# Reordering the first batch of an attention and feed-forward kernel: part one's plain products first, q and k of part two in one load each, two heads in other banks

## The chip, the cores and the metric

The kernel runs on one core of a Trainium2 chip. A core has TensorE (matrix products, results in PSUM), VectorE and ScalarE (elementwise work; both read PSUM), GpSimd and SyncE (here memory clearing and the issue of DMAs). PSUM has eight banks of 128 partitions by 512 float32 values. The metric is device time in microseconds (us) of one execution: the median of several runs. Lines of the profile call TensorE PE, VectorE DVE, ScalarE ACT, GpSimd POOL and SyncE SP; PEld is TensorE's load of weights.

## What is computed

Eight batches of eight heads attend over 576 tokens of 64 values, and a feed-forward network with a squared relu follows. Heads 0 to 3 ("plain") see the last 32 tokens; heads 4 to 7 ("dilated") see every fourth of the last 128.

```python
# B, H, S, D = 8, 8, 576, 64; window 32, dilation 4
scores = q @ k.T / sqrt(D)
rel = pos[:, None] - pos[None, :]
mask_plain = (rel >= 0) & (rel < 32)
mask_dil = (rel >= 0) & (rel < 128) & (rel % 4 == 0)
attn = softmax(where(mask_plain if h < 4 else mask_dil, scores, -1e9))
x = (attn @ v).transpose(0, 2, 1, 3).reshape(4608, 512)   # B*S tokens, H*D wide
h = maximum(x @ w_in, 0)                                  # w_in 512 x 2048
out = (h * h) @ w_out                                     # w_out 2048 x 512, float32
```

## The kernel before

Heads go in pairs e = 0 to 3 (two heads of 64 values fill 128 partitions); e = 0 and 1 are plain, 2 and 3 dilated. Tokens are grouped in fours: token 4m + r has residue r and index m, m from 0 to 143. Batch 0 is cut in two parts: part one (0 in the code) is m below 64, that is 256 tokens, part two (1 in the code) the other 320. The normalised attention output goes, transposed, into `xT`, whose 512 rows are four blocks kt = 0 to 3, one for each head pair. The feed-forward network takes tokens in tiles: four of 256, then 512 each.

Instructions are issued on each engine in the order in which the code writes them. For the start that order is written out by hand in the string `PROGRAM` (lines 21 to 36). It is cut by "|": all codes before the first "|" run ahead of the first group of feed-forward work, the codes of the next stretch after group 0, and so on. In the first stretch the codes mean, with e and part as digits:

- `L0:q023`, `L0:q10123`: load q and k of batch 0, a part and a list of head pairs, one DMA each from GpSimd (`load_qk`, line 156). `L0:v..` loads v, `L0:i` and `L0:o` quarters of w_in and w_out. A DMA issue on GpSimd waits for the landing of the one eight issues before it.
- `T`: transposes of q and k (line 505, into a tile `pa`). `C`: their copies out of PSUM, on VectorE, or for plain pairs with "a" the q half on ScalarE (lines 512 to 520); dilated pairs of part two have a small extra copy (`k8`, line 514).
- `B`: a product that puts the mask's bias in PSUM (line 535). `S`: scores (line 557). `E`: exponential on ScalarE (line 565), and for part two a product with the mask on VectorE (line 568).
- `h`: VectorE copies v of the plain heads of part one (tile `plain`, profile name `osb`, loaded from SyncE and ScalarE at line 745) to the place where it is used (line 803).
- `P`: the product with v (line 595). `D`: the sums of the exponentials (line 611). `L`, `X`: logarithm and exponential on ScalarE that give the reciprocal (lines 618 and 621). `M`: the product that normalises, on VectorE, into `xT` (line 628). For part one two head pairs share a pair of banks, and one `L`, `X`, `M` serves both.
- `wn`, `Wn`: n matrix products of zeros (line 475), whose results are not used; `W2+31` puts them on the bank of S31.

The four banks of the pool `ps_f` (profile name `pf`) serve B and S, some of P's results and the accumulators of the feed-forward network; `ps_a` has two banks (`pa`), `ps_o` and `ps_d` one each (`po`, `pd`). A tile that is allocated waits until the bank that it is given has been read for the last time.

A feed-forward tile is a list of groups (`ffn_groups`, line 653). A first-layer group g1(i) makes products over w_in (`mm1`, line 666; 676 in the profile), then ScalarE's relu (line 687) and VectorE's square (line 688); second-layer groups follow (line 711). For the tile of tokens 0 to 255, group 0 makes kt 0 and 1 of two accumulators and group 1 their kt 2 and 3. `P01` to `M31` of part two are issued after group 1. Then the groups of the first two tiles are interleaved: group 2 is the first of tokens 256 to 511 (g1(0)), groups 3 and 4 are g1(2) and g1(3) of tokens 0 to 255, group 5 is g1(1) of tokens 256 to 511, which completes the accumulators that group 2 began.

Of the kernel before, what the change touches and what calls it, by code (L numbers as in the profile page):

```python
# [18 lines left out]


PROGRAM = (
    "L0:q001 L0:q023 L0:q101 L0:q123 L0:v0d L0:i0 L0:v1p L0:v1dr L0:i1 L0:i2 L0:i3 L0:o0 L0:o1 L0:o2 L0:o3 "
    "L1:q00123 z y L1:v0dp L1:q10123 L1:v1dpr w9 T00 C00a T10 C10a B00 B10 W2 S00 E00 B20 W1 S10 E10 u B30 W3 "
    "T20q W6 T20k C20v T30 C30v h W3 S20 E20 W2 S30 E30 T01 C01v T11 C11a P00 P10 D00 D10 L00 T21 C21v T31 "
    "C31v S01 S11 X00 M00 E01 E11 P20 P30 D20 D30 L20 X20 M20 S21 S31 W2+31 E21 E31 | | P01 D01 L01 X01 M01 "
    "P11 D11 L11 X11 M11 P21 D21 L21 X21 M21 P31 D31 L31 X31 M31 | | | | | | | | | | | | | | | m n | | | | | "
    "L2:q00123 L2:q10123 | 1q1 1q3 | 1q2f 1k2f | 1k1a 1v3 | 1a2 | 1v2 1k0a 1q0v | 1o2 | 1a0 1a1 | 1k3 1o0 1o1f "
    "| 1a3 1Q0 | 1K0 1o3 | 1Q1 1K1 | 1Q2 | 1b0 | | 1Q3 1K2 L2:vwpdr L3:q00123 L3:q10123 | L2:x | | 2q0 | | 2k0 "
    "1V2 | 1b2 1p0 | 1b1 1V3 1K3 | | 1p2 1p1f | 2a0 1b3 | 2k1l 2o0 1p3f 2b0 2k1h | 2q1 2k2 L3:x | | 2q2 2p0 "
    "L3:vwpdr 2a1 | | | 2b1 | 2o1 2a2 2v2 2q3 | | 2p1f | 2k3 | 2b2 2o2 | 2v3 | 2a3 2p2f L4:q10123 | 2b3 2o3 | "  # L30
    "3k1 | 2p3 | 3q1v L4:q00123 | 3k0l | | 3a1 3k0h | | 3k2l | 3o1 3q0 | 3k2h 3v2 | | | 3a0 | 3b1 | 3q2 | | "
    "3p1 L4:x L4:vwpdr | | 3b0 | 3a2 3q3 3o0 3k3 | | | 3o2 3b2 | 4q1 | 3p0 3v3 | 3a3 | 3p2 4q2 4q0 | L5:q10123 "
    "3b3 4k0al | 3o3 4k0ah | 4k1 | | L5:q00123 3p3 4k2 4k3 4a0 L5:vwpdr | | | 4b0 | | 4q3 | | 4o0 | | | 4a2 "
    "4v2 | 4b2 | 4a3 L5:x 4a1 | 4o2 | | | 4p2 L6:q00123 4v3 | | 4b1 | | 4p0 | | 4p1 | 5q0 5k0 | 4b3 | | | | "
    "4o1 | | 5k2 L6:q10123 4o3 | 5q2 5k1 | | 4p3 | 5q1 |"
)


# [25 lines left out]
def kernel(  # L64
# [414 lines left out]
    def first_step(code: str):  # L479
# [6 lines left out]
        m0, n = MS[part], MN[part]  # L486
# [4 lines left out]
        pair = (e - e % 2, 0) if part == 0 else (e, 1)  # L491

        def byr(ap):
            return ap.rearrange("p (r m) -> p r m", r=RES)

        if what == "T":
# [3 lines left out]
            x = first["T", e, part]  # L500
# [7 lines left out]
        elif what == "C":  # L508
            copy = nc.scalar.copy if code[3] == "a" else nc.vector.tensor_copy
            x = first.pop(("T", e, part))  # L510
# [25 lines left out]
        elif what == "S":  # L536
# [7 lines left out]
            y = 0  # L544
            for x, (i, r, q0, q1) in enumerate(bl):
                z = (q1 - q0) * (RES if r is None else 1)
# [15 lines left out]
        elif what == "E":  # L562
            ps = first.pop(("S", e, part))
            to = pts[e][:, c : c + ps.shape[1]]
            nc.scalar.activation(to, ps, ACT.Exp, scale=SCALE)
            if part:
                mask = (mask_d if dil else mask_p)[:, c : c + ps.shape[1]]
                nc.vector.tensor_tensor(out=to, in0=to, in1=mask, op=ALU.mult)
        elif what == "P":
            if ("P", *pair) not in first:  # L570
                if pair in ((2, 0), (0, 1), (3, 1)):
                    od = ps_o.tile([P, 512], f32, name="po"), ps_d.tile([P, 512], f32, name="pd")
                else:
                    pool, nm = (ps_a, "pa") if pair == (1, 1) else (ps_f, "pf")
                    od = [pool.tile([P, 512], f32, name=nm) for _ in range(2)]
                first.pop("W", None)
                first["P", *pair] = od
            o, d = [x[:, y0 : y0 + w] for x in first["P", *pair]]
            o3, d3 = byr(o), byr(d)
            pt = pts[e]  # L580
            bl = blocks(0, e, part)
            y, dms = c, []
            for x, (i, r, q0, q1) in enumerate(bl):
                z = (q1 - q0) * (RES if r is None else 1)
                quads = dil and i < 8
                for rows in sides if quads else [slice(0, P)]:
                    if r is None:
                        to, rhs = o3[rows, :, q0 - m0 : q1 - m0], byr(pt[rows, y : y + z])
                    else:
                        to, rhs = o3[rows, r, q0 - m0 : q1 - m0], pt[rows, y : y + z]  # L590
                    if quads:
                        lhs = vds[0][rows, e - NE // 2, i // RES, D * (i % RES) : D * (i % RES) + D]
                    else:
                        lhs = vbd[0][:, e, i, :]
                    nc.tensor.matmul(
                        to, lhs, rhs, start=(x == 0 and y0 == 0), stop=(x == len(bl) - 1), skip_group_check=True
                    )
                if not dil:
                    dms.append((d3[:, :, q0 - m0 : q1 - m0], byr(pt[:, y : y + z])))
                y += z  # L600
            if dil and part == 0:
                dms.append((d, pt[:, 0:w]))
            elif dil:
                main = byr(pt[:, c : c + 448])
                dms += [(d3, main[:, :, 32:112]), (d3[:, :, 0:32], main[:, :, 0:32]),
                        (d3[:, :, 64:80], byr(pt[:, c + 448 : c + 512]))]
            first["D", e, part] = dms
        elif what == "D":
            dms = first.pop(("D", e, part))
            for x, (dd, rh) in enumerate(dms):  # L610
                nc.tensor.matmul(
                    dd, ones, rh, start=(x == 0 and y0 == 0), stop=(x == len(dms) - 1), skip_group_check=True
                )
        else:
            n = 512 if part == 0 else w
            if what == "L":
                first["X", e, part] = rec = r_pool.tile([P, 512], f32, name="rec")
                nc.scalar.activation(rec[:, 0:n], first["P", e, part][1][:, 0:n], ACT.Ln)
            elif what == "X":
                rec = first["X", e, part][:, 0:n]  # L620
                nc.scalar.activation(rec, rec, ACT.Exp, scale=-1.0)  # L621
            else:
                o, rec = first["P", e, part][0][:, 0:n], first.pop(("X", e, part))[:, 0:n]
                to = xT[:, e, RES * m0 : RES * m0 + n]
                if part == 0:
                    to = xT[:, e : e + 2, 0:w]
                    o, rec = [x.rearrange("p (e n) -> p e n", e=2) for x in (o, rec)]
                nc.vector.tensor_tensor(out=to, in0=o, in1=rec, op=ALU.mult)  # L628
# [24 lines left out]
    def ffn_groups(tk0: int, nt: int):  # L653
# [6 lines left out]
        kts = (0, 2, 1, 3) if tk0 >= NT else (0, 1, 2, 3)  # L660
# [5 lines left out]
        def mm1(u, ks):  # L666
            if u not in acc:
                acc[u] = ps_f.tile([P, NT], f32, name="pf")
            for x in range(per):
                f = per * u + x  # L670
                piece = max(y for y in range(len(w_in_sb)) if w_cuts[y] <= P * f)
                c0 = 512 * (f // 4) + f % 4 - w_cuts[piece]
                for kt in ks:
                    for y0, y1 in cuts:
                        t0 = (tk0 + y0) % RING
                        nc.tensor.matmul(  # L676
                            acc[u][:, nt * x + y0 : nt * x + y1],
                            w_in_sb[piece][:, kt, c0 : c0 + 509 : 4],
                            xT[:, kt, t0 : t0 + y1 - y0],
                            start=(kt == kts[0] and x == 0 and y0 == 0),  # L680
                            stop=(kt == kts[-1] and x == per - 1 and y1 == nt),
                            skip_group_check=True,
                        )
            if ks[-1] != kts[-1]:
                return
            hv = h2[:, per * u : per * u + per, 0:nt]
            nc.scalar.activation(hv, acc[u][:, :].rearrange("p (x n) -> p x n", x=per), ACT.Relu)  # L687
            nc.vector.tensor_tensor(out=hv, in0=hv, in1=hv, op=ALU.mult)  # L688

        def g1(i):  # L690
            if i < 2 and tk0 < NT:
                for u in range(2):
                    mm1(u, kts[2 * i : 2 * i + 2])
            elif i < 2 and early:
                for u in (2 * i, 2 * i + 1):
                    mm1(u, kts[:cut])
            elif i < 4 and early:
                for u in (2 * i - 4, 2 * i - 3):
                    mm1(u, kts[cut:])
            else:  # L700
                mm1(i, kts)
# [189 lines left out]
```

## Time and profile before

| | |
|---|---|
| Median of 4 runs | 310.98 us (309.46 to 312.5) |
| The profiled execution | 310.02 us, its span 308.2 us |
| TensorE busy | 300.6 us, 98% of the span |
| VectorE, ScalarE, GpSimd busy | 194.1, 198.7, 93.8 us |
| First product over w_in of group 0 | 17.69 us from the span's start |
| First product over w_in of group 2 | 22.66 us |

A line of the timeline gives start and length in us, engine, line of the code, operation, what it writes and reads, shapes and count; in brackets stands how long the engine had been idle before it and what ended that. A line of waits gives who waited for whom, the time in total, how often, and the longest. A line of GpSimd with DMA_DIRECT2D is the issue of a transfer; its landing is told apart. Starts of matmuls that follow each other without a gap overlap their ends by up to 0.2 us, so lengths of neighbours don't add up; differences of starts do.

### The profile page before, as it was taken

Reading aid. Unit: us, or ns where it says so; the run is one execution under the profiler, and the core shown is the slowest. Engines: PE = TensorE matmul, PEld = TensorE weight load, DVE = VectorE, ACT = ScalarE, POOL = GpSimd, SP = SyncE. Lnnn points to the kernel's source line nnn. Section 1 sums busy time; section 2 is a strip of 40 time slices with the busy share of each in tenths; the row PEclk is TensorE's granted clock in tenths of the full one; section 3 lists DMA queues with packets and bytes.
Section 4 is the critical chain, followed back from the end, with each engine's and each line's share of the span. In section 5 each row is a group of like instructions: output and inputs, shape, how many; then the busy total and the mean of one; then the engine's idle time right before and its main releaser. Section 6 shows DMA issues by size and latency. Waiting matters only on the chain.

```text
span 308.2 us, 6774 instructions
## 1 busy us (share of the span) xinstructions
PE 300.6 (98%) x2532; PEld 187.9 (61%) x2564; DVE 194.1 (63%) x635; ACT 198.7 (64%) x425; POOL 93.8 (30%) x138
## 2 busy tenths in 40 slices
PE   8999999999999999999999999999999999999995
PEld 3679757868755555555599555555555555445544
DVE  1465566988988888885798479946994334104400
ACT  6686658859869868894488448854786456216511
POOL 8679685574255165301641051000000000000000
PEclk9999999999999999999999999999999999999999
DMA  7999999999989979999899976502200210121022
GB/s 105 194 140 213 207 160 170 183 159 220 142 147 192 173 113 212 137 121 163 118 123 136 149 121 92 101 24 58 57 3 1 69 69 0 36 68 34 0 63 76
DMA packets 80288, 35.05 MB, mean 114 GB/s; under 512 B 49920, under 2 KB 75648, under 8 KB 80256
## 3 DMA queue, kind: packets, MB, share of 16 engines
q0 software_dynamic: 46592, 18.23, 52.8%
q1 hardware_dynamic: 32976, 16.06, 28.0%
q8 instruction: 20, 0.33, 0.5%
q10 hardware_dynamic: 688, 0.33, 0.5%
q14 instruction: 12, 0.10, 0.1%
HBM read 36.90 MB, written 9.44 MB: 150 GB/s over the span
## 4 chain that ended last, share of the span: by engine, by line
PE 93%; ACT 2%; DMA 1%; issue 1%; DVE 1%; POOL 0%; ACTq 0%; POOLq 0%
PE pf L676 40%; PE pf L711 40%; PE po L421 3%; PE pd L423 3%; PE pa L312 2%; PE pa L318 2%; PE pa L236 1%; DMA kb<-in_k_dram 1%; PE pa L505 1%; PE po L475 1%; ACT h2T L687 1%; PE pf L535 0%; PE pf L557 0%; DVE xT L628 0%; ACT rec L621 0%
## 5 line engine op out<-in xcount | busy, mean ns | idle before, releaser
L676 PE MATMUL pf<-xT,w_in 128*128 128x256 bf16 (+1 forms) x758 | 131.9, 325 | 0.7 <-DVE xT L628 0.2
L711 PE MATMUL pf<-w_out_sb,h2T 128*128 128x512 bf16 (+1 forms) x570 | 130.7, 373 | 1.2
L676 PEld LDWEIGHTS <-w_in 128*128 128x128 bf16 x768 | 82.4, 113 | 34.9 <-issue 0.3
L687 ACT ACTIVATE h2T<-pf 128x512 bf16<-128x512 f32 x144 | 83.9, 599 | 25.3 <-PE pf L676 24.5
L711 PEld LDWEIGHTS <-h2T 128*128 128x128 bf16 x592 | 54.3, 98 | 53.5
L688 DVE TENSOR_TENSOR h2T<-h2T 128x512 bf16<-128x512 bf16 x144 | 58.1, 423 | 40.6 <-ACT h2T L687 39.3
L718 ACT COPY osb<-pf 128x512 f32<-128x512 f32 (+1 forms) x37 | 21.0, 567 | 43.8 <-PE pf L711 40.9
L436 DVE TENSOR_TENSOR xT<-po,rec 128x288 bf16<-128x288 f32 (+2 forms) x51 | 23.2, 455 | 32.1 <-ACT rec L426 31.7
L178 POOL DMA_DIRECT2D vbd<-in_v_dram x36 | 25.7, 732 | 44.6 <-PE pd L423 39.6
L425 ACT ACTIVATE rec<-pd 128x288 f32<-128x288 f32 (+2 forms) x51 | 20.9, 410 | 20.6 <-PE pd L423 20.5
L322 ACT ACTIVATE pt<-pa 128x352 bf16<-128x352 f32 (+6 forms) x56 | 27.6, 499 | 6.4 <-PE pa L312 3.5
L426 ACT ACTIVATE rec<-rec 128x288 f32<-128x288 f32 (+2 forms) x56 | 24.8, 444 | 1.8
L421 PEld LDWEIGHTS <-vbd 128*128 128x128 bf16 x286 | 17.1, 97 | 9.4 <-issue 0.3
L256 DVE COPY qT<-xx 64x288 bf16<-64x288 bf16 x84 | 20.4, 243 | 1.2
L191 POOL DMA_DIRECT2D vd<-in_v_dram x24 | 14.6, 621 | 15.2 <-DMA kb<-in_k_dram 8.7
L161 POOL DMA_DIRECT2D qb<-in_q_dram x18 | 13.0, 720 | 19.1 <-DMA xx<-qb 17.3
L421 PE MATMUL po<-pt,vbd 128*128 128x32 bf16 (+3 forms) x256 | 17.5, 198 | 0.0
L260 DVE COPY kbd<-xx 64x288 bf16<-64x288 bf16 x36 | 16.9, 470 | 0.5
L423 PE MATMUL pd<-pt,mk 128*128 128x32 bf16 (+6 forms) x150 | 15.9, 204 | 0.0
L161 POOL DMA_DIRECT2D kb<-in_k_dram x18 | 12.6, 702 | 1.8 <-DMA w_in<-in_moe_w_in_dram 0.7
L197 POOL DMA_DIRECT2D vbd<-in_v_dram x16 | 9.6, 601 | 11.0 <-PE pd L423 5.1
L312 PE MATMUL pa<-qT,kbd 128*128 128x96 bf16 (+2 forms) x146 | 12.2, 201 | 0.0
(99 smaller groups left out, 240.7 us busy)
## 6 DMA issues: line engine op xcount, KB each, us to landing
out_dram<-osb SPq DMA_DIRECT2D x18, 128.0 KB, 2.5
qb<-in_q_dram POOLq DMA_DIRECT2D x7, 320.0 KB, 7.2
kb<-in_k_dram POOLq DMA_DIRECT2D x7, 320.0 KB, 9.2
vd<-in_v_dram POOLq DMA_DIRECT2D x32, 64.0 KB, 6.2
w_in<-in_moe_w_in_dram POOLq DMA_DIRECT2D x4, 512.0 KB, 7.8
w_out_sb<-in_moe_w_out_dram POOLq DMA_DIRECT2D x4, 512.0 KB, 14.5
qb<-in_q_dram POOLq DMA_DIRECT2D x7, 256.0 KB, 6.8
kb<-in_k_dram POOLq DMA_DIRECT2D x7, 256.0 KB, 8.4
```

The source lines that it names most:

```text
L161: nc.gpsimd.dma_start(t[0:n, part, hs, :], src[b, hs, t0 : t0 + RES * n, :].rearrange("h (p r) d -> p h (r d)", r=RES))
L178: nc.gpsimd.dma_start(dst[rows, e, i0:i1, rows], v[b, 2 * e + hl, 64 * i0 : 64 * i1, :].rearrange("(i p) d -> p i d", p=64),)
L322: nc.scalar.activation(pt[:, off : off + n], ps[:, 0:n], ACT.Exp, scale=SCALE)
L421: nc.tensor.matmul(oo, vb[:, e, i, :], rh, start=(x == 0), stop=(x == len(mms) - 1), skip_group_check=True)
L423: nc.tensor.matmul(dd, ones[:, :], rh, start=(x == 0), stop=(x == len(dms) - 1), skip_group_check=True)
L426: nc.scalar.activation(rec[:, 0:n], rec[:, 0:n], ACT.Exp, scale=-1.0)
L436: nc.vector.tensor_tensor(out=tok, in0=o if o is o3 else o[:, 0:n], in1=rec if o is o3 else rec[:, 0:n], op=ALU.mult)
L676: nc.tensor.matmul(acc[u][:, nt * x + y0 : nt * x + y1], w_in_sb[piece][:, kt, c0 : c0 + 509 : 4], xT[:, kt, t0 : t0 + y1 - y0], start=(kt ...
L687: nc.scalar.activation(hv, acc[u][:, :].rearrange("p (x n) -> p x n", x=per), ACT.Relu)
L688: nc.vector.tensor_tensor(out=hv, in0=hv, in1=hv, op=ALU.mult)
L711: nc.tensor.matmul(cur[m][:, c0:c1], h2[:, f, P * m : P * m + P], w_out_sb[:, f, c0:c1], start=(f == 0), stop=(f == NF - 1),)
L718: nc.scalar.copy(osb[:, c0:mid], cur[m][:, c0:mid])
```

## The change

Four things change, all in batch 0 or in the first groups after it:

- q and k of part two are loaded for all head pairs in one DMA each (`L0:q10123`), in place of two each.
- `P00 P10 D00 D10 L00 X00` come before `T01 C01v T11 C11a`, with four products of zeros (`W4`) between them; `P20 P30 D20 D30 L20` come after T11 and before T21. `M00 X20 M20` come after S11 and ahead of E01; before, X20 and M20 stood behind E01, E11 and D30.
- P of pair 2, part two, takes the banks `po` and `pd`; pairs 0 and 3 of part two take two banks of `ps_f` each. Before, pairs 0 and 3 had `po` and `pd` and pair 2 two of `ps_f`.
- Group 2 (tokens 256 to 511) makes kt 0 alone of its two accumulators, and group 5 kt 1, 2 and 3; before, it was kt 0 and 1, and kt 2 and 3.

All other codes of the string keep their order.

```diff
 PROGRAM = (
-    "L0:q001 L0:q023 L0:q101 L0:q123 L0:v0d L0:i0 L0:v1p L0:v1dr L0:i1 L0:i2 L0:i3 L0:o0 L0:o1 L0:o2 L0:o3 "
-    "L1:q00123 z y L1:v0dp L1:q10123 L1:v1dpr w9 T00 C00a T10 C10a B00 B10 W2 S00 E00 B20 W1 S10 E10 u B30 W3 "
-    "T20q W6 T20k C20v T30 C30v h W3 S20 E20 W2 S30 E30 T01 C01v T11 C11a P00 P10 D00 D10 L00 T21 C21v T31 "
-    "C31v S01 S11 X00 M00 E01 E11 P20 P30 D20 D30 L20 X20 M20 S21 S31 W2+31 E21 E31 | | P01 D01 L01 X01 M01 "
...
+    "L0:q001 L0:q023 L0:q10123 L0:v0d L0:i0 L0:v1p L0:v1dr L0:i1 L0:i2 L0:i3 L0:o0 L0:o1 L0:o2 L0:o3 L1:q00123 "
+    "z y L1:v0dp L1:q10123 L1:v1dpr w9 T00 C00a T10 C10a B00 B10 W2 S00 E00 B20 W1 S10 E10 u B30 W3 T20q W6 "
+    "T20k C20v T30 C30v h W3 S20 E20 W2 S30 E30 P00 P10 D00 D10 L00 X00 W4 T01 C01v T11 C11a P20 P30 D20 D30 "
+    "L20 T21 C21v T31 C31v S01 S11 M00 X20 M20 E01 E11 S21 S31 W2+31 E21 E31 | | P01 D01 L01 X01 M01 P11 D11 "
...
         elif what == "P":
             if ("P", *pair) not in first:
-                if pair in ((2, 0), (0, 1), (3, 1)):
+                if pair in ((2, 0), (2, 1)):
                     od = ps_o.tile([P, 512], f32, name="po"), ps_d.tile([P, 512], f32, name="pd")
                 else:
                     pool, nm = (ps_a, "pa") if pair == (1, 1) else (ps_f, "pf")
...
         def g1(i):
             if i < 2 and tk0 < NT:
                 for u in range(2):
-                    mm1(u, kts[2 * i : 2 * i + 2])
+                    mm1(u, kts[: 1 + (tk0 == 0)] if i == 0 else kts[1 + (tk0 == 0) :])
             elif i < 2 and early:
```

## The prediction

> **What bounds the kernel now.** I read the page first: busy shares, then the chain that ended last.
>
> ```profile
> span 308.2 us, 6774 instructions
> ...
> PE 300.6 (98%) x2532; PEld 187.9 (61%) x2564; DVE 194.1 (63%) x635; ACT 198.7 (64%) x425; POOL 93.8 (30%) x138
> ...
> PE 93%; ACT 2%; DMA 1%; issue 1%; DVE 1%; POOL 0%; ACTq 0%; POOLq 0%
> ```
>
> TensorE sets the end: a microsecond of it, or of its waiting, is a microsecond of the whole. Next its waits, over the whole span:
>
> ```profile
> PE po L595 <- DVE xT L628: 0.5, 1, 0.5
> PE pa L557 <- DVE k L514: 0.3, 1, 0.3
> PE pf L676 <- DVE xT L628: 0.2, 1, 0.2
> ```
>
> All lie in the first batch, which is all that the change touches. There is little to win: by the gaps between matmuls, 0.34 (part two's scores S01 wait for a copy), 0.11 (S11), 0.16 (group 1 waits for M20) and 0.45 (P31 waits until M01 has freed its bank), 1.06 us together. From 22.66 on TensorE has no gap over 0.07 us until the last stores (as the trace puts the ends of matmuls), so what it loses before then stays lost. The order of events, from TensorE's timeline:
>
> ```profile
> 9.04 0.85 PE L475 MATMUL po<-idle 128*128 128x256 bf16 x3
> 9.81 0.42 PE L505 MATMUL pa<-mk,qb 64*64 64x64 bf16 x8
> 10.17 0.83 PE L475 MATMUL po<-idle 128*128 128x256 bf16 x6
> ...
> 12.66 0.34 PE L505 MATMUL pa<-mk,qb 80*64 80x80 bf16 x8
> ...
> 13.36 0.49 PE L595 MATMUL pf<-pt,vbd 128*128 128x96 bf16 x8
> ...
> 18.89 1.03 PE L676 MATMUL pf<-xT,w_in 128*128 128x256 bf16 x8 [0.16 <-DVE xT L628]
> ...
> 22.01 0.46 PE L595 MATMUL po<-pt,vd 64*64 64x32 bf16 x16 [0.45 <-DVE xT L628]
> ```
>
> 12.66 is T01, 13.36 P00, 18.89 group 1, 22.01 P31. Last, VectorE and ScalarE, which feed them:
>
> ```profile
> 11.95 1.01 DVE L803 CAST vbd<-osb 64x512 bf16<-64x512 f32 x2
> ```
> ```profile
> 19.52 1.09 ACT L687 ACTIVATE h2T<-pf 128x512 bf16<-128x512 f32 x2 [0.44 <-PE pf L676]
> 20.49 0.44 ACT L618 ACTIVATE rec<-pd 128x320 f32<-128x320 f32 x1
> ...
> 23.00 0.42 ACT L618 ACTIVATE rec<-pd 128x320 f32<-128x320 f32 x1
> 23.45 0.47 ACT L621 ACTIVATE rec<-rec 128x320 f32<-128x320 f32 x1
> ```
>
> The first row (code h) puts v where P00 reads it; it ends at 12.97, and P00 starts 0.39 later, so it has slack now. The other rows are ScalarE's run of two relus, then logarithm and exponential for four head pairs, end to end: about 0.83 us a pair, L31 ending at 23.42, M31 on VectorE at 24.45.
>
> **The change part by part.**
>
> *Loads.* Two GpSimd issues of about 0.69 us go (nothing else on its queue or SyncE's is moved), so v0d and the first weights are issued up to 1.4 us sooner. Each issue waits for the landing eight issues earlier; the weights (7.94, behind a landing at 7.65) would wait for the first q (landed 4.58). The Trainium skill (DMA: Bandwidth & Descriptors, section Anatomy of one DMA — SWDGE (gpsimd) path) gives each such DMA about 2.0 us fixed plus bytes at 436 GB/s: four of 160 KB 9.5 us, two of 320 KB 5.5 us, 4 us gained. The row says otherwise: part two's four loads land at 10.06, 11.34, 12.22 and 13.15, 1.09 us apart behind the one before; they stream, and no fixed share is there to save. I take 0 for the last byte, k at about 13.15. What speaks against merging is that T01 then waits for all of k, 13.15 in place of 11.34; T01 comes at 14.3 below, so this is covered by 1.1 us. Without that cover it costs what k is late. Behind the first weights nothing moves: the second v1r load still waits for their landing (16.30), and w_in's second quarter follows it (landing 22.65, first used after 23). Either rule gives 0 for the sum.
>
> *P00 P10 D00 D10 first.* TensorE is free at 12.66, but P00 needs h: 12.97 + 0.05 for the signal, so 13.02 (0.36 us of new idling, the slack used up). P and D take 0.32 each, issue to issue: 13.66.
>
> *W4.* Four idle matmuls, 0.11 apart (10.17: six in 0.83, with 0.27 for the last), and about 0.2 of switching: T01 begins at 14.29, 1.63 later than now. By the skill's clock gate (TensorE: Matmul & The Clock Gate, section Part 1: The HAM clock gate) the clock falls only after an idle window of about 3.4 us, and no gap here comes near, so W4 buys nothing and costs 0.5 to 0.65. But that section also has the clock rise after about 3.4 us of sustained work, and the rows don't follow: the matmuls at 1.07 keep TensorE busy for 4.0 us, and still at 9.04 idle matmuls stand 0.21 apart, and 0.11 only from 10.17. So the rule isn't safe here and W4 may be insurance; I charge 0.6 and no clock effect.
>
> *T01, T11, P20, P30, D20, D30, T21, T31.* T01 and T11 0.31 each, then P20/P30 0.35 and D20/D30 0.32 with switching (16.07 to 16.74 now): T21 can start at 15.60. VectorE copies: C01 from 14.79, 0.72 for both halves, 15.51; C11's k half 15.54 to 16.03, which holds T31 to 16.08; C21 16.10, its k8 done at 16.72; C31 and k8, 17.25. Now these end at 15.23 and 15.76. So S01 starts at 16.78 and S11 at 17.30 (15.29 and 15.81 now): 1.5 us later, but with P20 and D20 (0.67) already behind. S21 and S31 with W2 take 0.3 + 0.3 + 0.35: group 0 at 18.50 (17.69 now).
>
> *M00, X20, M20.* VectorE: M00 17.28 to 17.97, M20 to 18.58 (18.83 now). Group 0 runs eight matmuls of 0.109, to 19.37; group 1 follows with no wait. Net: group 1 at 19.37 against 18.89, +0.48. The masks of E01 to E31 queue on VectorE behind M20, until about 19.9; P01 comes at 20.25, P31 at 22.0: covered.
>
> *Banks.* P31 no longer waits for M01: it gets the banks of group 0's accumulators (relus done at 20.6 and 21.1) and starts at 22.0, finished near 22.65, as now. So the 0.45 is won, and that pays back the 0.48. But ScalarE's run also starts 0.47 late (relus at 19.99): M01 22.43, L31 until 23.89, M31 until 24.92. And the pool of four banks gives out the one freed longest ago. I take that from the trace: group 3's first matmul (23.60) waits on ScalarE and group 4's (24.48) on VectorE, which fits L21 and M21 of the pair that has those banks now. In the new order groups 3 and 4 get P31's banks, freed by L31 and M31, the last of the run. That is the wait that takes the place of the one removed.
>
> *Group 2.* With kt 0 alone it is four matmuls, not eight: 22.65 to 23.09. Four go to group 5 (0.44 of work, moved, not saved). Group 3 waits from 23.09 for L31: 23.93, eight matmuls to 24.80. Group 4 waits for M31: 24.96, to 25.83. Group 5, twelve: 27.14. Now group 5 ends at 26.22 (two groups of 0.87 from 24.475). Sum: +0.92, all of it kept.
>
> The profiled execution took 310.02 us with its 308.2 span, so 310.9 is its expected successor; the median of the runs shown is 310.98, 0.96 above it, and so 311.9.
>
> **The rivals.**
>
> *The banks are free in time.* If groups 3 and 4 get other banks, 23.09 + 2 x 0.87 = 24.83, group 5 waits 0.1 for M31 and ends at 26.23: nothing lost. If the copies also run 0.4 ahead of my reckoning, 0.4 is gained: 310.6. Bounded below, since only 1.06 of waits exist and W4 costs half. Against it: the waits seen on groups 3 and 4.
>
> *v late for P00 (slower).* The loads of v that h reads go out from SyncE and ScalarE at 3.4 to 4.2 and land at 9.2 to 11.5; h begins at 11.95, so from a landing after 11.95 on each lateness moves P00, with everything behind it on TensorE. The fuller GpSimd queue shares the same engines; at worst v lands with k at 13.15, P00 starts 0.9 later: 312.8. For it: that queue is crowded. Against: 0.4 of slack.
>
> *The clock falls (over 1% slower).* Between 12.7 and 18.5 TensorE now has gaps, but of 0.3. If the new ones (before P00, before S01, S11, group 3) let the clock fall, small matmuls double (up to 3.3 us) and dense ones stand 0.21 apart until it returns: about +4, 315. It decides once the spacing leaves 0.109. Against: today's gap of 0.45 did nothing.
>
> *The merge does nothing* is my own reading of it.
>
> **How the numbers follow.** Forecast 0.62 (311.9; its own range 311.3 to 312.5, from signals and copies uncertain by some 0.6); banks free 0.22 (310.6); v late 0.11 (312.8); clock 0.05 (315). The four times shown run from 309.46 to 312.5, so a median may lie 0.7 off: 309.9 to 313.4, leaving out the clock. 1%, about what a measurement of this kernel can tell from no change, is 3.1 us: slower 0.06, faster 0.02 (no case reaches it), within 0.92.
>
> **What would show it.** P00 at 13.0, T01 at 14.3, S01 at 16.8, group 0 at 18.5 and group 1 right behind with no wait on xT; P31 without a wait; then two gaps ahead of main products, about 0.8 (after ScalarE's L618) and 0.2 (after L628), near 23.1 and 24.8. No such gaps, or idle matmuls 0.21 apart after 13, would make it wrong.

## The result, and the profile after

The changed kernel takes 312.17 us (median of 44 runs, 309.95 to 315.71), the kernel before beside it 310.92 us (63 runs, 309.35 to 313.85). The ratio is 1.0021, with a 95% interval of 1.0004 to 1.0038. The ratio leaves out runs more than 1.5% above the fastest of their kernel, here 12 of the 44 of the changed kernel, in all of which TensorE's clock fell, so the medians, 0.4% apart, say more of what a user meets.

312.17 is close to the 311.9 forecast. But it is a mixture that the forecast didn't have. By the mean granted clock of each run, the 44 fall into four groups: 19 at 0.999 or above with a median of 310.72; 8 at 0.993 to 0.995 with 312.17; 7 at 0.988 or 0.989 with 314.26; 10 at 0.983 or 0.984 with 314.83. These are 0, 1, 2 and 3 stretches of 3.4 us at half clock: 3.4 x 0.5 / 310 = 0.0055 each.

The profiled execution (314.78 us, span 313.0) is of the last group. Its page, the lines that answer to those shown of before, and its row of the clock:

```profile
span 313.0 us, 6779 instructions
...
PE 304.0 (97%) x2536; PEld 190.3 (61%) x2568; DVE 194.1 (62%) x635; ACT 199.2 (64%) x425; POOL 92.8 (30%) x136
...
PEclk9859999999999999999999999999999999999999
...
PE 92%; DMA 3%; ACT 1%; DVE 1%; issue 1%; SPq 0%; ACTq 0%
```

TensorE still bounds the kernel, but 3% of the chain is now DMA; the page's list by line puts all of it on `osb<-in_v_dram`, the load of part one's plain v. The second and third of forty slices of the clock are at 8 and 5 tenths. TensorE's waits over the whole span:

```profile
PE pf L595 <- DVE vbd L803: 1.6, 1, 1.6
PE po L475 <- DVE idle L735: 1.1, 1, 1.1
PE pf L676 <- ACT rec L618: 0.7, 1, 0.7
PE pa L557 <- DVE k L514: 0.2, 1, 0.2
```

P31's and group 1's waits on `xT` (0.5 and 0.2) are gone. In their place are 1.6 us in which P00 waits for v's copy (code h, line 803), and 0.7 in which group 3 waits for L31 (line 618). (The 1.1 is the start of the program.) Where that happens, from VectorE's and then TensorE's timeline:

```profile
12.29 0.50 DVE L803 CAST vbd<-osb 64x512 bf16<-64x512 f32 x1 [1.42 <-DMA osb<-in_v_dram]
```
```profile
12.85 0.49 PE L595 MATMUL pf<-pt,vbd 128*128 128x96 bf16 x8 [1.61 <-DVE vbd L803]
13.17 0.48 PE L611 MATMUL pf<-pt,mk 128*128 128x96 bf16 x8
13.48 0.97 PE L475 MATMUL po<-idle 128*128 128x256 bf16 x4
...
20.72 3.42 PE L676 MATMUL pf<-xT,w_in 128*128 128x256 bf16 x16
...
27.64 0.60 PE L676 MATMUL pf<-xT,w_in 128*128 128x256 bf16 x4 [0.67 <-ACT rec L618]
```

The last of v lands at 12.27; TensorE had nothing left at 11.2. Four idle matmuls at 13.48 then take 0.97, where six took 0.83 before: TensorE runs at half clock. Groups 0 and 1 (20.72) take 3.26 where they take 1.75 at full clock (below). The same stretches as a table (us, then TensorE's busy time in each; the granted clock is the figure after POOL's):

```profile
6.75:10.15 3.40, 3.40 (x66) 2.29 (x65) 0.64 (x3) 2.41 (x8) 2.54 (x4) 1.00 1.20 155
10.15:13.57 3.42, 1.81 (x38) 1.25 (x36) 1.22 (x4) 0.77 (x2) 0.66 (x1) 1.00 1.39 197
13.57:16.98 3.41, 3.41 (x67) 2.35 (x65) 1.21 (x3) 1.84 (x4) 1.82 (x4) 0.50 1.60 183
```

One stretch of 3.4 us with TensorE busy for 1.81, and the next runs at half. In this execution the clock stays there for three stretches, until 23.81.

### The profile page after: what moved, and what is told of

Same layout as the page of the kernel before. It is cut to its first block, busy times and chain, and to the rows that moved or that the text cites. A ratio compares the mean times of both kernels' runs of the same rounds, so it can differ in the third digit from the quotient of the medians.

```text
span 313.0 us, 6779 instructions
## 1 busy us (share of the span) xinstructions
PE 304.0 (97%) x2536; PEld 190.3 (61%) x2568; DVE 194.1 (62%) x635; ACT 199.2 (64%) x425; POOL 92.8 (30%) x136
## 4 chain that ended last, share of the span: by engine, by line
PE 92%; DMA 3%; ACT 1%; DVE 1%; issue 1%; SPq 0%; ACTq 0%
PE pf L676 40%; PE pf L711 39%; PE po L421 3%; DMA osb<-in_v_dram 3%; PE pd L423 3%; PE pa L312 2%; PE pa L318 1%; PE pa L236 1%; DMA mk<-mask_patterns 1%; PE pa L505 1%; PE pf L595 0%; PE pa L557 0%; PE po L595 0%; PE pf L557 0%; PE pf L421 0%
## 5 line engine op out<-in xcount | busy, mean ns | idle before, releaser
L676 PE MATMUL pf<-xT,w_in 128*128 128x256 bf16 (+1 forms) x758 | 133.5, 328 | 1.2 <-ACT rec L618 0.7
```

The lines of the kernel that those rows point to most:

```text
L676: nc.tensor.matmul(acc[u][:, nt * x + y0 : nt * x + y1], w_in_sb[piece][:, kt, c0 : c0 + 509 : 4], xT[:, kt, t0 : t0 + y1 - y0], start=(kt ...
```

## The experiments

Each ran beside the kernel before on one chip, in several rounds. A run is "lost" when its mean clock was under 0.997. Unless said, a kernel is the changed one with the edit shown. The kernel before, over the 204 runs with a clock on record: 52 lost; median of the others 310.33, of the lost 311.25.

### The changed kernel again

> The changed kernel again, unaltered, beside the others on one chip. Theory A (TensorE idles before P00 until v is copied, and the clock falls by one to three windows of 3.4 us): the clock is lost in 40 to 65 of 100 runs, those without loss have a median of 0.3 to 0.7 above those of the kernel before without loss, and the median of all is 311.5 to 312.5.

Measured: 9 of 22 lost; the others 310.95, the kernel before without loss 310.34 in the same rounds; median of all 311.50. With the first 44, 34 of 66 lost: 310.84 without, 314.56 with. This execution's profile (310.92 us, span 309.1) lost nothing, and so is the one to hold against the forecast's steps (the first row is S30):

```profile
10.63 0.31 PE L557 MATMUL pf<-xx 64*64 64x64 bf16 x8
11.79 0.49 PE L595 MATMUL pf<-pt,vbd 128*128 128x96 bf16 x8 [0.84 <-DVE vbd L803]
...
13.70 0.34 PE L505 MATMUL pa<-mk,kb 80*64 80x80 bf16 x8 [0.42 <-DMA kb<-in_k_dram]
...
14.80 0.44 PE L595 MATMUL po<-pt,vd 64*64 64x64 bf16 x15 [0.33 <-DMA vd<-in_v_dram]
...
16.68 0.94 PE L557 MATMUL pa<-xx 64*64 64x32 bf16 x24 [0.43 <-DVE k L514]
...
18.39 1.91 PE L676 MATMUL pf<-xT,w_in 128*128 128x256 bf16 x16
...
21.87 0.46 PE L595 MATMUL pf<-pt,vd 64*64 64x32 bf16 x16
...
23.86 3.38 PE L676 MATMUL pf<-xT,w_in 128*128 128x256 bf16 x28 [0.73 <-ACT rec L618]
```

From S01 on each step stands within 0.15 of its forecast: S01 16.68 (16.78), group 0 18.39 (18.50) with group 1 right behind, P31 21.87 without a wait (22.0), group 3 23.86 after a wait for L31 (23.93), group 4 24.89 after M31 (24.96).

Ahead of S01 it is otherwise: P00 came 1.23 and T01 (12.95) 1.34 earlier than forecast, and that lead was gone by S01 because T01 waited for k and P20 for the dilated v.

The second layer begins at 35.80 against 34.95 before, +0.85 where +0.92 was forecast. But single executions of the old order differ by more than that (below, 34.15 and 35.28), so the closeness of this pair proves little.

### Idle matmuls ahead of P00

```diff
-S30 E30 P00 P10
+S30 E30 W14 P00 P10
```

> The changed kernel with 14 idle matmuls of 256 columns put ahead of P00 (about 1.5 us at 0.109 us each), nothing else. Theory A: the clock is lost because TensorE sits idle before P00 while it waits for v (1.61 us in the profile after). Then the granted clock is 0.998 or more in nearly all runs, no run is near 314.8, and the median is 310.5 to 311.5 (where v comes early the filling costs up to 1.0 us). Theory B: the clock falls because of the small matmuls of the new order, wherever the idling is. Then about half of the runs still show 0.993, 0.989 or 0.984, and the median is 312 to 313.

Measured: 0 of 22 lost; median 311.13, ratio 1.0022 (1.0006 to 1.0038). In its profile v was late as well:

```profile
10.76 1.70 PE L475 MATMUL po<-idle 128*128 128x256 bf16 x14
13.18 0.49 PE L595 MATMUL pf<-pt,vbd 128*128 128x96 bf16 x8 [0.71 <-DVE vbd L803]
13.50 0.48 PE L611 MATMUL pf<-pt,mk 128*128 128x96 bf16 x8
13.81 0.60 PE L475 MATMUL po<-idle 128*128 128x256 bf16 x4
```
```profile
11.00:14.42 3.42, 2.71 (x38) 2.08 (x37) 0.84 (x2) 0.66 (x2) 0.86 (x2) 1.00 1.34 200
14.42:17.83 3.41, 3.01 (x114) 2.42 (x116) 2.76 (x8) 2.81 (x6) 2.03 (x4) 1.00 1.43 141
```

P00 comes later here (13.18) than in the profile after (12.85), and the clock holds: the stretch with the wait has 2.71 us of work in place of 1.81. That settles theory A against B: the same small matmuls follow, and nothing is lost, where e4_banks_back lost 12 of 22 in the same rounds with no filling ahead of P00. The filling takes the lost clock away, not the wait for v: the median is still 0.7 above the kernel before (310.43). One run took 316.52 at full clock, against the expectation that none would come near 314.8; nothing on record says why.

### Part two's loads split again

```diff
-L0:q10123
+L0:q101 L0:q123
```

> The changed kernel with q and k of part two in two loads each again. If the merged loads make v late (landing 12.27 after, 11.51 before), v lands by 11.6, the idling before P00 is under 0.5 us, the clock is lost in under 1 run of 10 and the median is 310.5 to 310.9. If the new order alone brings the loss, whatever the loads, v lands late as often and about half of the runs are at 0.993 or lower, median 311.8 to 312.5.

Measured: 6 of 22 lost, median 310.70, without loss 310.37; ratio 1.0009 (0.9992 to 1.0027). The losses halve, to the share of the kernel before, but don't vanish, and the idling before P00 in the profile is 1.19, with v landing at 11.36. Neither expectation fits wholly. 6 of 22 against 34 of 66 is suggestive, not more. In this profile group 3 waits for a load that no step of the forecast has:

```profile
PE pf L676 <- DMA w_in<-in_moe_w_in_dram: 0.9, 1, 0.9
```

L31 is through at 22.82 here, and the second quarter of w_in lands at 23.02 (23.08 in e0_after, 22.65 before). So a head that runs sooner finds that load as the next bound.

### The merged loads alone

The kernel before, with this edit only:

```diff
-L0:q101 L0:q123
+L0:q10123
```

> The kernel before with the merged loads alone (old order, old banks). T01 then waits for the whole of k, landing at 13.2 to 13.5, where TensorE is through with S30 at 11 to 12.7: idling of 0.5 to 2.5 us. Theory A: the clock is lost in half of the runs or more here too, median 312 or more. If idling of this kind does not matter, the cost is the late T01 alone, 0.3 to 1 us: 311.2 to 311.9, clock 0.998 or more.

Measured (6 runs): 5 lost, median 314.33, ratio 1.0103 (1.0064 to 1.0141), the worst of all. TensorE's waits:

```profile
PE pa L505 <- DMA kb<-in_k_dram: 1.8, 1, 1.8
PE po L475 <- DVE idle L735: 1.1, 1, 1.1
PE pa L505 <- DMA qb<-in_q_dram: 0.7, 1, 0.7
```

In the old order T01 waits for all of q and all of k, 2.6 us, and its stretch of 3.4 us (11.77 to 15.18) has 1.58 us of TensorE work before the clock falls. The new order covers most of that wait (0.42 for k is left in e0_after), and pays with P00's.

The same with `W18` ahead of T01:

> The kernel before with the merged loads and 18 idle matmuls (1.97 us) ahead of T01. Theory A: it is the idling that loses the clock where the loads are merged (5 of 6 runs without filling), so now it is lost in under 1 run of 10. What is left is T01 waiting for k at about 13.5: 0.5 to 1.5 above the kernel before, 311.1 to 312.1. If merging loses the clock otherwise, losses stay in more than half.

Measured: 2 of 22 lost, median 311.32, without loss 311.31 against 310.46 of the kernel before: merge and filling together cost 0.85 at full clock when T01 comes first, and the rest of the harm above is the clock. What the merge alone costs at full clock, one run of e3_merge_only shows (311.62), too few to tell.

### The old order filled

The kernel before, with this edit only:

```diff
-S30 E30 T01
+S30 E30 W6 T01
```

> The kernel before with 6 idle matmuls (0.65 us) ahead of T01, nothing else. Theory A: the kernel before loses its clock too (34 of 126 runs so far) where TensorE idles ahead of T01 until q and k land; filled, it is lost in under 1 run of 10, and the median goes from 310.5 to 310.2-310.4. Where TensorE had no gap, the filling costs up to 0.65. If the loss in the kernel before comes from elsewhere, it stays at a quarter and the median rises to 310.8 or more.

Measured: 2 of 22 lost, median 310.52 against 310.60, ratio 1.0001 (0.9986 to 1.0016). Losses fall, with e11_fill_banks below to 3 in 36 runs against 52 in 204. The time, expected at 310.2 to 310.4, doesn't measurably: a loss costs this kernel only 0.9 us, and the filling is paid in every run. In this profile the old order begins its second layer much sooner than in the profile before, which stands first here:

```profile
34.95 6.21 PE L711 MATMUL pf<-w_out_sb,h2T 128*128 128x512 bf16 x27
```
```profile
34.15 6.21 PE L711 MATMUL pf<-w_out_sb,h2T 128*128 128x512 bf16 x28
```

### The new order alone

The kernel before with the new string except for the loads; banks and groups as before.

> The kernel before with the new order of codes alone (W4 included): loads, banks and the split of group 2 as before. By the prediction's steps group 1 comes 0.48 later, P31's wait for M01 stays: 0.4 to 0.6 above the kernel before without loss of clock, 310.6 to 310.8. Clock lost in a quarter of the runs, as with the loads split (6 of 22) and in the kernel before (16 of 59). If the order itself makes v's wait worse, in half of the runs.

Measured (14 runs): 8 lost, median 311.03; without loss 310.71 (6 runs) against 310.34, +0.37; ratio 1.0012 (0.9985 to 1.0039). The cost at full clock is near what the steps give (0.4 to 0.6), but six runs can't tell it from none. The losses are more than in e2_split, which differs from it in banks and groups only, in too few runs to say why. Its profile shows the clock fall after P00 waited 1.18:

```profile
8.97:12.39 3.42, 2.24 (x56) 1.54 (x55) 1.60 (x4) 1.38 (x5) 1.49 (x3) 1.00 1.41 194
12.39:15.80 3.41, 3.41 (x65) 2.71 (x62) 0.84 (x3) 1.65 (x3) 2.73 (x5) 0.50 1.42 196
```

### The old banks

```diff
-if pair in ((2, 0), (2, 1)):
+if pair in ((2, 0), (0, 1), (3, 1)):
```

> The changed kernel with the old banks: heads 0 and 3 of part two in po and pd, heads 2 in two banks of pf. By the step on banks the wait ahead of group 3 (0.67 us in the profile after, on L31) goes, P31 waits for M01 again (0.45), and the whole is 0.2 to 0.6 us faster than the changed kernel at equal clock. If the banks matter in no way, equal within 0.2. The clock is lost as often as in the changed kernel by every theory.

Measured: 12 of 22 lost; without loss 310.66, 0.49 above the kernel before in the same rounds (310.17), where the changed kernel stands 0.61 above in its own. In the profile the wait ahead of group 3 is gone and P31's is back:

```profile
PE pf L595 <- DVE vbd L803: 1.3, 1, 1.3
PE po L475 <- DVE idle L735: 1.1, 1, 1.1
PE pa L236 <- DMA kb<-in_k_dram: 0.6, 1, 0.6
PE po L595 <- DVE xT L628: 0.5, 1, 0.5
```

So the banks move a wait; the 0.2 to 0.6 expected in the time is not seen, and the 0.1 found is less than these runs can tell.

The new banks in the old order, filled as above:

> The kernel before with 6 idle matmuls ahead of T01 and the new banks alone (old order, old loads, old split of group 2). If ScalarE's run from relu 0 to L31 and M31 sets when groups 3 and 4 may start, the wait of P31 (0.45) goes and comes back ahead of group 3 or 4: no faster than with the filling alone, within 0.2. If the banks were the bound, 0.4 faster: 310.1. Clock lost in under 1 run of 10.

Measured (14 runs): 1 lost, median 310.59 against 310.57; ratio 0.9992 (0.9971 to 1.0014). Second layer at 35.28. P31 starts without a wait, and the time comes back at once:

```profile
22.23 0.28 PE L676 MATMUL pf<-xT,w_in 128*128 128x256 bf16 x1
22.93 5.30 PE L676 MATMUL pf<-xT,w_in 128*128 128x256 bf16 x45 [0.42 <-DVE xT L628]
```

That wait is within group 2, for M11 (kt 1), ahead of the place that was expected. So ScalarE's run of relus, logarithms and exponentials is the bound, and the banks only say where TensorE waits for it. That is read from the trace; the interval of the times alone would leave room for the 0.4 of the other expectation.

### Group 2 as before

```diff
-mm1(u, kts[: 1 + (tk0 == 0)] if i == 0 else kts[1 + (tk0 == 0) :])
+mm1(u, kts[2 * i : 2 * i + 2])
```

> The changed kernel with group 2 making kt 0 and 1 again and group 5 kt 2 and 3. By the step on group 2 the four matmuls (0.44 us) fill part of the wait ahead of group 3, which shrinks from 0.67-0.72 to about 0.25: 0.3 to 0.45 us faster than the changed kernel at equal clock. If group 3 waits for something else (the second quarter of w_in), equal within 0.2. Clock lost as often as in the changed kernel.

Measured: 14 of 22 lost; without loss 310.39 (8 runs) against 310.95 of the changed kernel in the same rounds: 0.56 faster, where 0.3 to 0.45 was expected, though so few runs leave even the sign open. Its profile, of a lost run, has 0.42 of waiting for M11 in place of the 0.7. The direction of the step on group 2 holds there, and in the next two versions.

### Two versions mended

New order and banks, loads split, `W8` ahead of P00 in place of W4, group 2 as before:

> New order and new banks, but the loads in two each, 8 idle matmuls ahead of P00 in place of W4 behind it, and group 2 with kt 0 and 1 again. If idling before P00, the late v and the moved four matmuls are what the change costs, the clock is lost in under 2 of 22 runs, and the median is 309.9 to 310.4, at or below the kernel before. If something else in the order costs as well, 310.7 or more.

Measured: 7 of 22 lost; without loss 310.27 against 310.34; median 310.56 against 310.60, ratio 1.0000 (0.9974 to 1.0025). At full clock no extra cost is left that these runs can tell. But the clock falls as often as before the change, where under 2 of 22 was expected: in its profile TensorE waits 1.29 for part one's dilated v ahead of P20 (landing 14.99 and 15.20), and the clock falls at the end of that stretch, at 16.14.

Merged loads, `W10` ahead of P00 and W2 behind, group 2 as before:

> The changed kernel (merged loads, new order, new banks) with 10 idle matmuls ahead of P00 and two behind it in place of four, and group 2 with kt 0 and 1 again. Both faults that the runs show are mended: the clock is lost in under 1 run of 10, group 3 waits 0.3 or less; median 310.2 to 310.7, no worse than the kernel before within 0.2. If there is a further cost, 311 or more.

Measured: 5 of 22 lost, median 310.94 against 310.60; ratio 1.0008 (0.9988 to 1.0028). Fewer than in the changed kernel, more than with fourteen ahead and four behind (none), and more than the 1 in 10 expected; without loss 310.52 against 310.57. So the three versions with group 2 as before (this, e7_split_fill_kts, e5_kts_back) stand within 0.1 of the kernel before at full clock, over 40 runs without loss, where the changed kernel stands 0.61 above; two of them have filling ahead of P00 as well. No version is measurably faster than the kernel before.

## Why the prediction was right, and where it wasn't

**Right: nothing to win, and the stall moves.** Of 1.06 us of waits at most, none was kept. ScalarE's run began 0.39 later (relu at 19.91 against 19.52), and group 3 waited 0.73 for L31 and group 4 for M31, at the places and for the releasers named. At full clock that is +0.85 in the head of e0_after and +0.51 in the medians (310.84 against 310.33) where +0.92 was summed, so the sum was too large by about 0.4. The medians of all runs are 1.25 apart because the clock falls more often than before (34 of 66 runs, against 52 of 204) and costs more where it does. The rule of the bank freed longest ago fits: groups 3 and 4 waited for L31 and M31.

**Right: the shift stays.** From the start of the second layer to the end of the span it is 273.3 us in the profile before and in e0_after alike.

**Wrong: "TensorE is free at 12.66", and with it the slack of v.** That was read from an execution in which TensorE got its full clock only at 10.20, as the spacing of its idle matmuls tells (0.21, then 0.11); the clock figures of stretches and runs don't count the start. S30 stood late there:

```profile
12.42 0.31 PE L557 MATMUL pf<-xx 64*64 64x64 bf16 x8
```

In the thirteen others profiled the full clock came between 3.9 and 7.0: those with the new order were through with S30 at 10.7 to 11.8, and then idled for v. The cold start had hidden v's lateness. So the wait ahead of P00 is 0.8 to 1.6 where nothing fills it, not 0.36, and v's slack of 0.39 was no property of the kernel.

**Wrong: "I take 0" for the loads, in part.** k lands at 13.49 and 13.66 in the two profiles of the changed kernel, 0.3 to 0.5 after the 13.15 taken (13.49 to 14.90 over the eight with merged loads). In e0_after T01 comes at 12.95, and so k isn't covered: T01 waits 0.4 for it, and P20 0.3 for the dilated v. This error and the one before run against each other: TensorE was ahead, and the loads held it back. That S01 still met its time within 0.1 is luck. v's last landing was 12.27 and 11.28 in the two profiles of the changed kernel. Whether the merge itself makes v late stays open: it is 11.21 to 12.74 in the six profiles with loads split (median 11.52) and 11.28 to 13.14 in the eight with loads merged (12.10).

**Wrong in size: the clock, at 0.05.** It falls in 34 of 66 runs, and costs 3.7 us where it does (310.84 to 314.56), close to the +4 priced. The forecast held against it that a gap of 0.45 had done nothing; the gap to weigh was the one before P00, which it had put at 0.36. The rival "v late" is not a case beside the clock but its cause: the two should have been one case, and a likely one. By luck of the mixture the median of all runs lies in between, and so near the forecast.

**W4.** It was charged 0.6 as possible insurance. It stands behind the wait for v, and only filling ahead of that wait insured (e1_fill). Nor did it cost 0.6 in e0_after: T01 waited there for k, which landed at 13.66, and would have waited for it without W4 too.

## What to carry to other kernels

Read a gap off one execution only after asking what else in it may move: here TensorE's clock came 3 to 6 us later in the profiled run than in the thirteen others, and that gave v its slack. When work is moved ahead of a slower producer, price the idling twice, as time and as clock, and put any filling ahead of the wait, as much as covers it. And when a wait is removed by another bank, follow the engine that fed the old wait: if it is the bound, the wait comes back one or two groups on.

## What the runs showed that was not expected

The clock doesn't need a stretch that is idle throughout to fall. In the profiles it changes at multiples of 3.41 us, with a phase that differs from execution to execution (first full clock at 3.90 to 10.20). Stretches at full clock with 1.58, 1.81, 2.13, 2.14 and 2.24 us of TensorE work (e3_merge_only, the profile after, e7_split_fill_kts, e5_kts_back, e8_order_only) were followed by half clock. But one in e0_after was not:

```profile
11.17:14.58 3.41, 2.27 (x53) 1.75 (x53) 0.92 (x3) 1.64 (x4) 1.29 (x3) 1.00 1.34 202
14.58:18.00 3.42, 2.66 (x105) 2.17 (x107) 2.68 (x8) 2.30 (x5) 2.05 (x4) 1.00 1.37 134
```

so the bound lies near two thirds of a stretch by this measure. Two more, of 61% (e4_banks_back) and 67% (e2_split), also passed, so busy time as modelled orders them only roughly. The Trainium skill (TensorE: Matmul & The Clock Gate, section Part 1: The HAM clock gate, What's actually happening) has the clock fall after an idle window of about 3.4 us; the length agrees, the idling needed does not: 1.18 us of waiting, placed wholly within one stretch (e8_order_only), was enough. Since the phase differs from one execution to the next, the same wait falls within one stretch in one run and across two in another: P00's lay wholly in one in the profile after (11.24 to 12.85, in 10.15 to 13.57) and across a change of stretch in e0_after (10.94 to 11.79, change at 11.17). That this is why one kernel loses the clock in half of its runs fits the profiles; it is not shown for each run.

Nor is it shown why the full clock came so late in the profile before. In its stretch from 3.38 to 6.79 TensorE was busy for 3.32 us, and the clock rose only at 10.20; in e0_after 3.27 us in the stretch from 0.93 to 4.34 were enough.
